# Block sums and the value products of batch 0 on the whole array, in a sparse-attention and expert-mixture kernel

## The chip, the cores and the metric

The kernel runs on one core of one Trainium2 chip. The metric is the device time of one execution in microseconds. Before the change it is 678.07 us, the median of three runs from 675.09 to 680.74 us. The profiled execution is one more execution, and its page gives its span, from the first to the last instruction: 673.4 us.

## The reference

Two things are computed one after the other. First comes attention for 4 batches of 8 heads with 768 positions of 64 numbers: every query sees its neighbours within 15 positions, and beside them 24 summaries, one for each block of 32 keys, whose value is the mean of the block's values.

```python
k_sum = k.reshape(B, H, nb, block, D).max(axis=3)      # block = 32, nb = 24
v_sum = v.reshape(B, H, nb, block, D).mean(axis=3)
scores_l = scale * np.matmul(q, k.transpose(0, 1, 3, 2))
mask_l = np.abs(pos[:, None] - pos[None, :]) < 16
scores_s = scale * np.einsum('bhsd,bhnd->bhsn', q, k_sum) + np.log(block)
a = softmax of [where(mask_l, scores_l, -1e9), scores_s]
out = a @ concatenate([v, v_sum])
```

Its output, 3072 rows of 512, goes through eight experts of 1024 hidden units. A gate of eight numbers a row is normalised eight times by rows and by columns and weighs the experts:

```python
P = np.exp(logits - logits.max())
for _ in range(8):
    P /= P.sum(1, keepdims=True); P /= P.sum(0, keepdims=True); P *= N / E
for e in range(8):
    out += P[:, e:e + 1] * (np.maximum(x @ w1[e], 0.0) @ w2[e])
```

## The kernel before, in words

**Stages.** The kernel has three stretches. The first does the attention together with expert 0 (`hidden0` and `project0`, lines L200 and L210), the second is a bridge with the normalisation of the gate (`sink`, L1117) and the first groups of expert 1, and the third goes through experts 1 to 7 in a loop written out by hand (L907 and L913). The change touches the first stretch alone, and by its planner also the bridge.

**Units.** Attention works on 16 pairs of heads, four for each batch, and 768 positions are six tiles of 128. Pairs 0 to 3 (batch 0, `PB` = 4) go in two halves of three tiles each (`pair_half`), all others as a whole (`pair_whole`). The steps of a pair are: keys and queries are transposed into `tkq` (L302 and L289 for batch 0, L305 later, and by DMA for the last pairs), copied out as `kT` and `qT` (L196); block maxima of the keys, `ksT` (L328); scores in `sg` (L334, in two PSUM banks of which there is one set), exponential on ScalarE (L458, L377), a band mask on VectorE (L463 and L468, later L383); scores of the summaries in `ss` (L420, L430) and their exponential (L441); block sums of the values in `vs` (L342), copied into `Vs` or `Ve` (L349); the value products in `av` (L479, later L406 and L412); normalisation (L509, L510); a transpose into `tx` (L517) and a copy into `xT` (L196), which is what expert 0 and the gate read.

**Shapes on TensorE.** Most products use 128 rows and 128 columns of the array. Some use a part: the scores have a contraction of 64, so that the two heads lie in two row halves (64x128); the transposes of batch 0 and `vs` put out 64 columns (128x64); `ss` is 64x32. The value products of one half pair in batch 0 (`values_h`) take three forms: six products of 128x128 for the tiles themselves, ten of 32x32 for the edges (the last or first 32 keys of a neighbouring tile against the first or last 32 queries), and three of 64x128 for the summaries. Each adds into the same bank `av`.

**Order.** A planner, class `Plan`, writes the instructions of all engines in the order of a list schedule: each unit has a cost on its engine, a list of units that it depends on, a priority and the PSUM buffers that it opens. Of the units that could start within 0.02 us of the earliest, the one with the lowest priority number goes first. Attention comes before expert 0, whose units fill what is left of TensorE; until the first unit of expert 0 is done, idle time of TensorE is filled with products of zeros (`keep_busy`, L555). Each engine then executes its own queue strictly in that order. The loads of q, k, v and weights all go out on GpSimd's queue, the transposes by DMA and the neighbour values (L362, L364) on SyncE's. `constants` is one unit on VectorE at the start; it is followed there by the identity and the band, of which GpSimd makes the rest (L572, L565, L567) between two loads.

Of the kernel before, what the change touches and what calls it, by code (L numbers as in the profile page):

```python
# [18 lines left out]
class Unit:  # L19
# [3 lines left out]
    def __init__(self, eng, cost, fn, deps, prio, opens, lag):  # L23
        self.eng = eng if isinstance(eng, dict) else {eng: cost}
        self.fn, self.deps, self.prio, self.opens, self.lag = fn, deps, prio, opens, lag
        self.start = self.end = self.on = None
# [7 lines left out]
class Plan:  # L34

    HOP = 0.15

    def __init__(self, slots, idle=None):
        self.slots, self.idle = {}, idle
        self.ring, self.turn, self.free, self.waiting = {}, {}, {}, []  # L40
        self.more(slots)
# [5 lines left out]
    def add(self, eng, cost, fn, deps=(), prio=0.0, opens=(), uses=(), lag=0.0):  # L47
        u = Unit(eng, cost, fn, [d for d in deps if d is not None], prio, list(opens), lag)
        for b in list(opens) + list(uses):
            b.users.append(u)  # L50
        if uses and eng != "PE":
            u.prio -= 100.0
        self.waiting.append(u)
        return u

    def order(self):
# [13 lines left out]
        while waiting or left:  # L70
# [4 lines left out]
            for u in left:  # L75
                t0 = ready(u)
                if t0 is None:
                    continue
                for e, cost in u.eng.items():
                    t = max([t0, free.get(e, 0.0)]  # L80
                            + [d.end + d.lag + (self.HOP if d.on != e else 0.0) for d in u.deps])
                    best.setdefault(e, []).append((t, u, cost))
            picks = []
            for e, c in best.items():
                t_min = min(t for t, _, _ in c)
                t, u, cost = min((x for x in c if x[0] <= t_min + 0.02), key=lambda x: x[1].prio)
                picks.append((t, t + cost, e, u, cost))
            t, end, e, u, cost = min(picks, key=lambda x: x[:2])
            if self.idle is not None:
# [3 lines left out]
                while self.idle is not None and t > free.get("PE", t) + us:  # L93
# [9 lines left out]
                    x.on = "PE"  # L103
# [4 lines left out]
            free[e] = end  # L108
            for b in u.opens:
                ring[b.tag][turn[b.tag] % self.slots[b.tag]] = b  # L110
                turn[b.tag] += 1
# [5 lines left out]
def kernel(  # L117
# [23 lines left out]
    W = 16  # L141
    LIVE = 128 + 2 * W
    PADL = LIVE + 2 * W
    HS = S // 2
    HG = G // 2
    VD = D + 1
    NEH = 3
# [78 lines left out]
    if True:  # L226
# [4 lines left out]
        m_blk = attn.tile([128, G, 64], BF16, name="m_blk")  # L231
# [4 lines left out]

        E_h = [attn.tile([128, 2, HG + 1, PADL], BF16, name=f"Eh{i}") for i in range(NEH)]
        V_s = [attn.tile([64, 2 * VD], BF16, name=f"Vs{i}") for i in range(PB)]
# [98 lines left out]

        def block_sums(i):
            sv = v_x[i % NQ]
            vs = at["vs", i] = bank("a", "vs")[0:64, 0:2 * D]  # L340
            for g in range(G):
                nc.tensor.matmul(vs.rearrange("p (j d) -> p j d", j=2), lhsT=m_blk[:, g, :],  # L342
                                 rhs=sv[:, :, g, 0:D], start=(g == 0), stop=(g == G - 1))
# [13 lines left out]
        def near_values(i):  # L357

            sv, ve = v_x[i % NQ], V_e[i % NE]
            for j in range(2):  # L360
                c0, q0 = VD * j, 64 + 32 * j
                nc.sync.dma_start(out=ve[q0 + W:q0 + 2 * W, 1:G, c0:c0 + VD],  # L362
                                  in_=sv[128 - W:128, j, 0:G - 1, :])
                nc.sync.dma_start(out=ve[q0:q0 + W, 0:G - 1, c0:c0 + VD],  # L364
                                  in_=sv[0:W, j, 1:G, :])
# [34 lines left out]
        def values(i, h):  # L400
            sv, ee, ve, em = v_x[i % NQ], E_e[i % NE], V_e[i % NE], at["em", i]
            av = at["av", i, h] = bank("a", "av")
            for cc in range(HG):
                c, o = HG * h + cc, cc * 2 * VD
                for j in range(2):
                    nc.tensor.matmul(av[:, o + j * VD:o + (j + 1) * VD],  # L406
                                     lhsT=em[:, j, c, :], rhs=sv[:, j, c, :],
# [26 lines left out]
        def summary_exp(i, h):  # L434
            o = 64 * h if i >= PB else 0
            if i < PB:
                es = at["es", i, h] = attn.tile([64, HG, 128], BF16, tag="es", name="es", bufs=2)
                dst = es[:]
# [21 lines left out]

        def masks_h(i, h):
            er, em = at.pop(("er", i, h)), E_h[(PB * h + i) % NEH]
            nc.vector.tensor_tensor(  # L463
                out=em[:, :, 0:HG, W:W + LIVE],
                in0=er[:, :, 0:HG * LIVE].rearrange("p j (g l) -> p j g l", l=LIVE),
                in1=band[:, None, None, :].to_broadcast([128, 2, HG, LIVE]), op=ALU.mult)
            p0, l0 = ((0, 0), (96, LIVE - W))[h]
            nc.vector.tensor_tensor(  # L468
                out=em[p0:p0 + 32, :, HG, W + l0:W + l0 + W],
                in0=er[p0:p0 + 32, :, HG * LIVE:HG * LIVE + W],  # L470
                in1=band[p0:p0 + 32, None, l0:l0 + W].to_broadcast([32, 2, W]), op=ALU.mult)

        def values_h(i, h):
            sv, em, es = v_x[i % NQ], E_h[(PB * h + i) % NEH], at.pop(("es", i, h))
            av = at["av", i, h] = bank("a", "av")

            def mm(p0, p1, cc, j, lhsT, rhs, n=VD, start=False, stop=False):
                o = cc * 2 * VD + j * VD
                nc.tensor.matmul(av[p0:p1, o:o + n], lhsT=lhsT, rhs=rhs, start=start, stop=stop,  # L479
                                 skip_group_check=True)  # L480

            for cc in range(HG):
                for j in range(2):
                    mm(0, 128, cc, j, em[:, j, cc, 2 * W:2 * W + 128], sv[:, j, HG * h + cc, :],
                       start=(cc == 0 and j == 0))
            for cc in range(HG):
                c = HG * h + cc
                for j in range(2):
                    if c + 1 < G:
                        mm(96, 128, cc, j, em[0:32, j, cc + 1, 0:32], sv[0:32, j, c + 1, :])  # L490
                    if c > 0:
                        mm(0, 32, cc, j, em[96:128, j, cc - 1 if cc else HG, LIVE:PADL],
                           sv[96:128, j, c - 1, :])
            for cc in range(HG):
                mm(0, 128, cc, 0, es[:, cc, :], V_s[i][:], n=2 * VD, stop=True)


        def normalize(i, h):
            av = at.pop(("av", i, h))[:, 0:HG * 2 * VD].rearrange("p (c x) -> p c x", x=VD)
# [6 lines left out]
            if i >= PB:  # L506
                t = t[:, HG * h:HG * (h + 1), :, :]
            rc = attn.tile([128, G, 1], FP32, tag="rc", name="rc", bufs=2)
            nc.vector.reciprocal(out=rc[:, :, 0], in_=av[:, :, D])  # L509
            nc.vector.tensor_tensor(out=t.rearrange("p g j d -> p (g j) d"), in0=av[:, :, 0:D],  # L510
                                    in1=rc[:].to_broadcast([128, G, D]), op=ALU.mult)
# [64 lines left out]

        def constants():
# [9 lines left out]
            for t in E_h:  # L587
                nc.vector.memset(t[:, :, :, 0:W], 0.0)
                nc.vector.memset(t[:, :, :, W + LIVE:], 0.0)
# [3 lines left out]
            for pq in range(4):  # L593
                for o in (pq, 32 + pq):
                    nc.vector.memset(flat[32 * pq:32 * pq + 32, o:o + 68 * (G - 1) + 1:68], 1.0)
# [41 lines left out]
        def pair_start(i, prio):  # L637
# [4 lines left out]
            for z in range(2 if i >= PB else 1):  # L642
                if i >= 12:
# [7 lines left out]
                                    prio, opens=[buf])  # L651
# [7 lines left out]
            U["vs", i] = add("PE", 0.4, lambda: block_sums(i),  # L659
# [4 lines left out]
        def query_half(i, h, prio):  # L664
# [3 lines left out]
                                opens=[buf])  # L668
# [4 lines left out]
        def pair_half(i, h, prio):  # L673
            if h:
                query_half(i, 1, prio)
            n = PB * h + i
            hold = U["A", PB - 1, 0] if h else None
            buf = Buffer("s")
            U["S", i, h] = add("PE", 0.36, lambda: scores_h(i, h),
                               [U["kT", i, 0], U["kT", i, 1], hist("mk", n - 3), hold], prio, opens=[buf])  # L680
            U["X", i, h] = add("ACT", 1.0, lambda: score_exp_h(i, h), [U["S", i, h]], prio, uses=[buf])
            U["mk", i, h] = add("DVE", 0.78, lambda: masks_h(i, h),
                                [U["X", i, h], U["band"], hist("A", n - NEH)], prio)
# [3 lines left out]
                                [U["km", i], U["kT", i, 1], hist("A", n - 2), hold], prio, opens=[buf])  # L687
            U["sx", i, h] = add("ACT", 0.46, lambda: summary_exp(i, h), [U["ss", i, h]], prio, uses=[buf])
            buf = Buffer("a")
            U["A", i, h] = add("PE", 0.65, lambda: values_h(i, h),  # L690
# [11 lines left out]
        def pair_whole(i, prio):  # L702
            U["near", i] = add("SP", 2.5, lambda: near_values(i), [U["v", i], U.get(("A", i - NE, 1))], prio,
                               lag=1.9)
            for h in range(2):
                buf = Buffer("s")
                U["S", i, h] = add("PE", 0.28, lambda h=h: scores(i, h),
                                   [U["kT", i, 0], U["kT", i, 1], U.get(("ed", i - 2))], prio, opens=[buf])
# [6 lines left out]
            U["ss", i, 0] = U["ss", i, 1] = add("PE", 0.22, lambda: summaries2(i),  # L715
                                                [U["km", i], U["kT", i, 1], U.get(("A", i - NE, 1))], prio,
                                                opens=bufs)
# [3 lines left out]
            for h in range(2):  # L721
                buf = Buffer("a")
                U["A", i, h] = add("PE", 0.4, lambda h=h: values(i, h),
# [570 lines left out]
```

## Time and profile before

| | |
|---|---|
| median of three runs | 678.07 us (675.09 to 680.74) |
| span of the profiled execution | 673.4 us |
| TensorE busy | 663.9 us, 99% of the span |
| VectorE busy | 580.2 us, 86% |
| ScalarE busy | 402.5 us, 60% |
| GpSimd busy | 131.5 us, 20% |
| granted TensorE clock | 0.999 over the span |
| first product of expert 0 (L200) starts at | 25.34 us |
| first product of L913 (end of the bridge) starts at | 168.68 us |

The span is 4.6 us under the median of the runs; the page does not give that execution's own device time, so a difference worked out in the span is carried over to the median as it stands. Matmuls are pipelined: a row's mean time is the time of one matmul from issue to end, several of them overlap, and the cost of a stream is read from the distance between the starts.

### The profile page before, as it was taken

The page shows a single profiled execution, that of the slowest core. Times are in us where ns is not written, and L with a number is a line of the kernel's source. Part 1 is how long each engine was busy: PE and PEld are TensorE (multiplying, and loading weights), DVE is VectorE, ACT ScalarE, POOL GpSimd, SP SyncE. Part 2 cuts the span into 40 slices and gives each one's busy share as a digit, 9 for nine tenths or more (in the row PEclk, how much of TensorE's full clock was granted, in tenths as well). Part 3 has the DMA queues.
Part 4 walks back from the last instruction along what each step waited for, and adds up shares of the span by engine and source line. Part 5 has one row for each costly group of instructions (what it writes and reads, how often), then busy time and mean ns, then how long its engine had stood idle before and what let it go on. Part 6 is the DMA issues. An engine that isn't in the chain of part 4 may idle for free.

```text
span 673.4 us, 13531 instructions
## 1 busy us (share of the span) xinstructions
PE 663.9 (99%) x5111; PEld 434.8 (65%) x5111; DVE 580.2 (86%) x1433; ACT 402.5 (60%) x783; POOL 131.5 (20%) x177
## 2 busy tenths in 40 slices
PE   8999999999999999999999999999999999999996
PEld 4666655555666666666666666666666666666665
DVE  6878889777799988998899988998899889998885
ACT  4777776565777765555655565555555555556552
POOL 8599622122101010201010010101020101100001
PEclk9999999999999999999999999999999999999999
DMA  9999959000513060311422050405031141201224
GB/s 115 190 147 145 151 85 172 2 1 1 79 11 37 1 79 1 36 14 21 59 22 28 1 78 9 40 1 79 1 33 17 20 60 20 30 0 48 82 91 158
DMA packets 124018, 36.46 MB, mean 54 GB/s; under 512 B 110384, under 2 KB 121136, under 8 KB 123952
## 3 DMA queue, kind: packets, MB, share of 16 engines
q0 software_dynamic: 104672, 26.22, 41.8%
q1 hardware_dynamic: 18464, 8.83, 5.6%
q8 instruction: 40, 0.66, 0.4%
q10 hardware_dynamic: 816, 0.54, 0.2%
q14 instruction: 26, 0.21, 0.1%
HBM read 52.45 MB, written 6.29 MB: 87 GB/s over the span
## 4 chain that ended last, share of the span: by engine, by line
PE 93%; DVE 4%; DMA 1%; POOL 1%; issue 1%; ACT 0%; DVEq 0%; ACTq 0%
PE xy L913 36%; PE pg L907 16%; PE pa L907 11%; PE pb L907 11%; PE hps L200 6%; PE yps L210 6%; PE sg L334 1%; DMA kst<-in_k_dram 1%; DVE hf L857 1%; PE tkq L305 1%; PE vs L342 1%; PE av L406 1%; PE av L412 1%; PE ss L430 1%; PE tx L517 0%
## 5 line engine op out<-in xcount | busy, mean ns | idle before, releaser
L913 PEld LDWEIGHTS <-hf 128*128 128x128 f16 x2352 | 230.1, 98 | 95.6 <-issue 0.5
L913 PE MATMUL xy<-w,hf 128*128 128x256 f16 x1312 | 183.4, 273 | 0.0
L913 PE MATMUL xy<-ws,hf 128*128 128x256 f16 x984 | 147.6, 273 | 0.1
L191 ACT ACTIVATE hf<-pg 128x512 f16<-128x512 f32 x84 | 50.2, 597 | 150.8 <-PE pg L907 150.8
L1049 DVE SCALAR_TENSOR_TENSOR out_acc<-xy,P_sb,out_acc 128x512 f32<-128x512 f32 x164 | 115.1, 744 | 2.1 <-PE xy L913 2.1
L854 DVE TENSOR_TENSOR hf<-hf 128x512 f16<-128x512 f16 x252 | 100.3, 424 | 8.8
L907 PE MATMUL pa<-xT,w 128*128 128x512 f16 x336 | 99.9, 379 | 0.0
L907 PEld LDWEIGHTS <-w 128*128 128x128 f16 x672 | 65.8, 98 | 44.4 <-issue 1.1
L857 DVE TENSOR_TENSOR hf<-pb,c 128x512 f16<-128x512 f32 x84 | 58.1, 692 | 38.5 <-PE pb L907 32.4
L176 POOL DMA_DIRECT2D w<-in_moe_w_dram x56 | 41.7, 754 | 220.6 <-PE pg L907 192.0
L907 PEld LDWEIGHTS <-ws 128*128 128x128 f16 x504 | 49.3, 98 | 25.3
L941 ACT COPY c<-pg 128x512 f32<-128x512 f32 x84 | 49.2, 586 | 22.4 <-PE pg L907 22.4
L857 DVE TENSOR_TENSOR hf<-pg,c 128x512 f16<-128x512 f32 x84 | 57.2, 681 | 0.8 <-PE pg L907 0.8
L926 ACT COPY pg<-pa 128x512 f32<-128x512 f32 x84 | 47.9, 570 | 4.8
L191 ACT ACTIVATE hf<-pa 128x512 f16<-128x512 f32 x84 | 50.6, 602 | 0.0
L907 PE MATMUL pg<-xTs,w 128*128 128x512 f16 x168 | 50.0, 379 | 0.2
L907 PE MATMUL pg<-xT,w 128*128 128x512 f16 x168 | 50.0, 379 | 0.1
L907 PE MATMUL pb<-xT,ws 128*128 128x512 f16 x168 | 50.0, 379 | 0.0
L907 PE MATMUL pb<-xTs,ws 128*128 128x512 f16 x168 | 50.0, 379 | 0.0
L907 PE MATMUL pg<-xTs,ws 128*128 128x512 f16 x168 | 50.0, 379 | 0.0
L934 ACT COPY c<-pb 128x512 f32<-128x512 f32 x84 | 49.8, 592 | 0.0
L200 PE MATMUL hps<-xT,w 128*128 128x384 f16 x256 | 48.6, 326 | 0.0
(141 smaller groups left out, 820.1 us busy)
## 6 DMA issues: line engine op xcount, KB each, us to landing
w<-in_moe_w_dram POOLq DMA_DIRECT2D x8, 1024.0 KB, 8.9
w<-in_moe_w_dram POOLq DMA_DIRECT2D x56, 128.0 KB, 3.5
out_dram<-out_acc SPq DMA_DIRECT2D x20, 256.0 KB, 2.0
qst<-in_q_dram POOLq DMA_DIRECT2D x32, 96.0 KB, 5.7
vx<-in_v_dram POOLq DMA_DIRECT2D x16, 192.0 KB, 6.5
kst<-in_k_dram POOLq DMA_DIRECT2D x24, 96.0 KB, 5.9
w<-in_moe_w_dram POOLq DMA_DIRECT2D x2, 512.0 KB, 8.6
kst<-in_k_dram POOLq DMA_DIRECT2D x4, 192.0 KB, 5.1
```

The lines of the kernel that those rows point to most:

```text
L176: nc.gpsimd.dma_start(out=t[:, :, h, :], in_=moe_w1[e].rearrange("(dk p) f -> p dk f", p=128)[:, :, f:f + 128])
L191: nc.scalar.activation(out=out, in_=in_, func=AF.Relu, bias=0.0, scale=1.0)
L200: nc.tensor.matmul(hp[:, 0:n], lhsT=w1s[e][:, dk, 128 * f:128 * (f + 1)], rhs=xT[:, dk, t0:t0 + n], start=(dk == 0), stop=(dk == KD - 1))
L210: nc.tensor.matmul(yp[:], lhsT=h[:, f, c * 128:(c + 1) * 128], rhs=w2s[e][:, f, :], start=(f == 0), stop=(f == KF - 1))
L854: nc.vector.tensor_tensor(out=out, in0=in0, in1=in1, op=ALU.subtract)
L857: nc.vector.tensor_tensor(out=out, in0=in0, in1=in1, op=ALU.add)
L907: nc.tensor.matmul(bank[:], lhsT=w[:, dk, :], rhs=x[:, dk, :], start=start and dk == 0, stop=dk == KH - 1, skip_group_check=True)
L913: nc.tensor.matmul(bank, lhsT=a(f)[:, 128 * c:128 * (c + 1)], rhs=w[:, f, :], start=start and f == 0, stop=f == FH - 1, skip_group_check=True)
L926: nc.scalar.copy(out=B["g"][:], in_=B["a"][:])
L934: nc.scalar.copy(out=B["c5"][:], in_=B["b"][:])
L941: nc.scalar.copy(out=B["c2"][:], in_=B["g"][:])
L1049: nc.vector.scalar_tensor_tensor(out=acc, in0=src, scalar=P_sb[:, t, e:e + 1], in1=acc, op0=ALU.mult, op1=ALU.add)
```

## The change

Three parts. First, the block sums (`block_sums`) get a 0/1 matrix `m_blk` of 128 columns instead of 64, so that their product is 128x128; rows 64 to 127 of the result are not read. Second, `values_h` computes everything with 128x128 products: the masked scores `E_h` get 112 zero columns around each stretch of 160 live ones, and an edge product takes a window of 128 columns in which only the live end is not zero, over all 128 keys of the neighbouring tile; the exponentials of the summaries go into two lasting tiles `E_s` whose lower half is zero, and `V_s` gets 128 rows. The zeros are written once, by `pads`: for the first of the three `E_h` tiles within `constants`, for the two others as units of their own on VectorE. The edge mask covers 128 partitions instead of 32. Third, units on TensorE carry a shape, the planner adds `RESHAPE` = 0.1 us to a unit whose shape differs from that of the last one, and of units that are ready together it takes one with a shape after another one with a shape; some costs are set anew. `normalize` is written with other views of the same data.

```diff
+    RESHAPE = 0.1
...
                 for e, cost in u.eng.items():
+                    if e == "PE" and u.shape != self.shape:
+                        cost += self.RESHAPE
...
-                t, u, cost = min((x for x in c if x[0] <= t_min + 0.02), key=lambda x: x[1].prio)
+                t, u, cost = min((x for x in c if x[0] <= t_min + 0.02), key=lambda x: (
+                    not (e == "PE" and self.shape and x[1].shape), x[1].prio))
...
-    PADL = LIVE + 2 * W
+    PAD = 128 - W
+    ROW = PAD + HG * (LIVE + PAD) + W + PAD
...
-        m_blk = attn.tile([128, G, 64], BF16, name="m_blk")
+        m_blk = attn.tile([128, G, 128], BF16, name="m_blk")
...
-        E_h = [attn.tile([128, 2, HG + 1, PADL], BF16, name=f"Eh{i}") for i in range(NEH)]
-        V_s = [attn.tile([64, 2 * VD], BF16, name=f"Vs{i}") for i in range(PB)]
+        E_h = [attn.tile([128, 2, ROW], BF16, name=f"Eh{i}") for i in range(NEH)]
+        E_s = [attn.tile([128, HG, 128], BF16, name=f"Es{i}") for i in range(2)]
+        V_s = [attn.tile([128, 2 * VD], BF16, name=f"Vs{i}") for i in range(PB)]
...
-            vs = at["vs", i] = bank("a", "vs")[0:64, 0:2 * D]
+            vs = at["vs", i] = bank("a", "vs")[:, 0:2 * D]
...
+        def live(c):
+            return PAD + c * (LIVE + PAD)
+
...
             for cc in range(HG):
                 for j in range(2):
-                    mm(0, 128, cc, j, em[:, j, cc, 2 * W:2 * W + 128], sv[:, j, HG * h + cc, :],
-                       start=(cc == 0 and j == 0))
+                    mm(cc, j, live(cc) + W, HG * h + cc, start=(cc == 0 and j == 0))
...
                     if c + 1 < G:
-                        mm(96, 128, cc, j, em[0:32, j, cc + 1, 0:32], sv[0:32, j, c + 1, :])
+                        mm(cc, j, live(cc + 1) + W - 128, c + 1)
                     if c > 0:
-                        mm(0, 32, cc, j, em[96:128, j, cc - 1 if cc else HG, LIVE:PADL],
-                           sv[96:128, j, c - 1, :])
+                        mm(cc, j, live(cc - 1) + W + 128 if cc else live(HG), c - 1)
             for cc in range(HG):
-                mm(0, 128, cc, 0, es[:, cc, :], V_s[i][:], n=2 * VD, stop=True)
+                o = 2 * cc * VD
+                nc.tensor.matmul(av[:, o:o + 2 * VD], lhsT=E_s[(PB * h + i) % 2][:, cc, :], rhs=V_s[i][:],
+                                 start=False, stop=True, skip_group_check=True)
...
+        def pads(n):
+            t = E_h[n]
+            nc.vector.memset(t[:, :, 0:PAD], 0.0)
+            nc.vector.memset(t[:, :, live(0):live(HG)].rearrange("p j (g l) -> p j g l", l=LIVE + PAD)[:, :, :, LIVE:],
+                             0.0)
+            nc.vector.memset(t[:, :, live(HG) + W:], 0.0)
...
-            for t in E_h:
-                nc.vector.memset(t[:, :, :, 0:W], 0.0)
-                nc.vector.memset(t[:, :, :, W + LIVE:], 0.0)
+            pads(0)
+            for t in E_s:
+                nc.vector.memset(t[64:128, :, :], 0.0)
...
+            clear = add("DVE", 0.65, lambda: pads(n), [c0], prio - 0.5) if 0 < n < NEH else None
...
-                               [U["kT", i, 0], U["kT", i, 1], hist("mk", n - 3), hold], prio, opens=[buf])
+                               [U["kT", i, 0], U["kT", i, 1], hist("mk", n - 3), hold], prio, opens=[buf], shape="row")
...
-            U["A", i, h] = add("PE", 0.65, lambda: values_h(i, h),
+            U["A", i, h] = add("PE", 0.67, lambda: values_h(i, h),
```

## The prediction

> **What bounds the kernel.** I read the page's busy times and its chain first. TensorE is busy 99% of the span and makes up 93% of the chain that ended last.
>
> ```profile
> PE 663.9 (99%) x5111; PEld 434.8 (65%) x5111; DVE 580.2 (86%) x1433; ACT 402.5 (60%) x783; POOL 131.5 (20%) x177
> ...
> PE 93%; DVE 4%; DMA 1%; POOL 1%; issue 1%; ACT 0%; DVEq 0%; ACTq 0%
> ```
>
> Busy time alone can hide gaps, since a matmul's end is modelled, so I asked next what TensorE waited for from the first product of expert 0 (25.34 us) to the end of the bridge (168.68 us):
>
> ```profile
> PE sink L1117 <- DVE csum_sb L1112: 0.8, 1, 0.8
> PE ss L430 <- DVE xT L196: 0.5, 1, 0.5
> ```
>
> The columns are total, times and longest. Two waits, 1.3 us of 143. There TensorE's queue is the bound: every nanosecond of TensorE work removed comes off the end, and everything that follows (pure matmul work as well) moves up. Before 25.34 us it is different: TensorE waits for loads and for other engines, and fills with zero products, so work removed there is worth nothing.
>
> Third, the timeline of TensorE in a piece of the middle stretch (start, busy, line, operation, count; a stream's cost is the distance to the next start):
>
> ```profile
> 41.56 1.89 PE L210 MATMUL yps<-w,h 128*128 128x512 f16 x8
> 43.39 0.38 PE L334 MATMUL sg<-qT,kT 64*128 64x160 bf16 x6
> 43.70 0.53 PE L342 MATMUL vs<-vx,m_blk 128*64 128x128 bf16 x6
> 44.16 1.04 PE L210 MATMUL yps<-w,h 128*128 128x512 f16 x4
> 45.03 0.35 PE L406 MATMUL av<-vx,em 128*128 128x65 bf16 x6
> 45.22 0.34 PE L412 MATMUL av<-Ve,Ee 128*128 128x130 bf16 x3
> ```
>
> Four `yps` products before `av`, same shape, take 45.03 - 44.16 = 0.87 us, 0.217 each; eight before `sg`, which has another shape, take 1.83, that is 0.09 more than 8 x 0.217. The single starts of the trace say it more sharply: `hps` to `hps` 162 ns, `hps` to `sg` 258; `yps` to `yps` 216, to `ss` 309; `vs` to `yps` 151, where two products of 128 elements stand 56 apart. **A change of shape costs 0.095 us**, whichever the two shapes are.
>
> **The changed work on TensorE.** I counted changes of shape in the order of instructions of both programs up to the end of the bridge: 141 before, 105 after. From the first product of expert 0 on, where they count, there are 100 and 72. So 28 x 0.095 = -2.66 us. One half pair of batch 0 shows where the fewer come from:
>
> ```profile
> 31.68 0.65 PE L479 MATMUL av<-vx,Eh 128*128 128x65 bf16 x16
> 32.26 0.34 PE L479 MATMUL av<-Vs,es 64*128 64x130 bf16 x3
> 32.53 1.47 PE L200 MATMUL hps<-xT,w 128*128 128x384 f16 x8
> ```
>
> From 31.68 to 32.53 three shapes follow each other, with a change before the ten edges, after them, and before `hps`.
>
> The edges get dearer. Nine distances between the ten 32x32 products make 172 ns, 19 each. The padded ones are 128x128 with 65 columns out, each with weights of its own, which is L406's form: 29 to 30 ns apart over 120 neighbours. Four of eight half pairs lie behind 25.34 us: 40 x 10.5 ns = +0.42 us. The three summary products stay at some 59 ns.
>
> The block sums: 72 products lie behind 25.34 us. Starts within `vs` are 62 ns apart on the mean, while `tx` with 128x128 and 128 elements shows 56. So 0 to -0.4 us; I take -0.2, the middle. The weight load of `vs` (64 columns) lasts 108 ns in the trace, that of 128 columns 98. The Trainium skill's page "TensorEngine Tiling (Array Packing)", under Restrictions, says that column tiling switches the fast weight load off, which would explain that odd order. By that rule the whole -0.4 would come, and the sum would be 0.2 us lower.
>
> One score unit now stands ahead of the first product of expert 0 instead of behind it: -0.30 us (a half pair's scores, 31.09 to 31.41 in the timeline).
>
> TensorE work behind the first product of expert 0: -2.66 + 0.42 - 0.2 - 0.30 = **-2.74 us**.
>
> **Waits there.** The first `sink` waits 0.8 us because only four expert products (0.65 us) stand between the start of the bridge and it. In the new order it is four and twelve more (0.65 + 2.59 us), so I take -0.8. The 0.5 us at `ss` may go or come back elsewhere: bounds 0 and -1.3 together. New waits are a rival below.
>
> **The start.** Here the change adds. GpSimd's second load stands in its queue behind the making of the identity, which waits for VectorE:
>
> ```profile
> 4.71 0.29 POOL L572 TENSOR_SCALAR_AFFINE_SELECT ident<-ident 128x128 bf16<-128x128 bf16 x1 [0.70 <-DVE ident L571]
> 4.95 0.72 POOL L262 DMA_DIRECT2D kst<-in_k_dram  x1
> ```
>
> VectorE clears the identity at 4.52 us, directly after `constants`. That unit gets longer. The rows: a memset of 384 words (L604) lasts 378 ns, one of 192 (L591) 218, so 0.83 ns a word and about 22 ns more from start to start; the six old ones of `E_h` stand 75 ns apart, 0.45 us together. Added are 560 words in three (0.53 us), two of 192 for `E_s` (0.36) and 192 more for `m_blk` (0.16): 1.05 - 0.45 = +0.60 us. All of GpSimd's later loads are issued 0.60 us later. How much of that reaches the keys of pair 3, the last of batch 0, is not in the trace: their arrival releases TensorE at 17.70 us,
>
> ```profile
> 17.70 0.53 PE L302 MATMUL tkq<-ident,kst 128*64 128x128 bf16 x12 [0.45 <-DMA kst<-in_k_dram]
> ```
>
> and the load was issued at 10.49, so for 7 us the DMA engines and not the issue were behind. Bounds 0 and 0.6; I take 0.4, as the first loads have been done by the time the second one's packets start. The other two `pads` (1.06 us) stand on VectorE where it idles from 5.23 to 6.64, and hold up the first query copy by some 0.4 us; the next keys are awaited anyway, so 0.
>
> From those keys to the first product of expert 0 there is a chain: transpose, copy, scores, exponential, mask, values, normalisation, transpose, copy. Before it takes 25.34 - 17.70 = 7.64 us. The new order puts three things into it: pair 3's queries are copied on ScalarE behind the key copy (0.80) instead of beside it on VectorE: 0.5 us; a copy into `xT` (0.3 to 0.36) stands ahead of the mask, partly in a wait; and the last copy into `xT`, here ahead of two query copies (the two lines of VectorE)
>
> ```profile
> 25.19 0.29 DVE L196 COPY xT<-tx 128x384 f16<-128x384 f16 x1
> 25.40 1.00 DVE L196 COPY qT<-tkq 128x384 bf16<-128x384 bf16 x2
> ```
>
> comes behind both, +1.1 us, of which TensorE has less to wait because that copy is read only by the fourth product. I take +1.2 us for the chain; bounds 0.3 (only the score unit that now runs in it) and 1.9 (all three in full). The start costs 0.4 + 1.2 = **+1.6 us**, between 0.3 and 2.5.
>
> **Edits at nothing.** The edge mask over 128 partitions: its time goes by elements per partition, which stay 32 (154 to 172 ns). `normalize`: same elements out of PSUM (557 ns). SyncE: one key transpose (1.21 us) now goes ahead of four neighbour loads (0.59 each) whose reader is far behind, two other moves are among transposes; TensorE's waits name no such DMA, and without that cover it would be 1.2 us. GpSimd's queue keeps its order.
>
> **The sum.** -2.74 - 0.8 + 1.6 = -1.94 us on the profiled span of 673.4, and so on the median of 678.07: **676.1 us**. With all terms at one end: -2.66 + 0.42 - 0.30 - 0.4 - 1.3 + 0.3 = -3.9 (674.1), and -2.54 + 2.5 = 0 (678.0). The runs of before scatter by -3.0 and +2.7 us around their median, so 1% (6.8 us) is about what a measurement tells from no change.
>
> **Rivals.**
>
> A. The start costs nothing beyond the 0.3 us and both waits go: -2.74 - 1.3 + 0.3 = -3.7, **674.3 us**. For it: VectorE idles in the chain for DMA. Against: the copy order, which is fixed in the queue. 13%.
>
> B. Slower: scores wait. There is one set of score banks (`NS` = 1), so a score unit needs the exponential of the last one finished (0.31 + 0.97 us and the two hand-overs, about 1.6). With the instruction order and the distances above, successive score units stand 1.7 us apart or more before; after, the closest late in attention are 1.59, 1.64, 1.69 and 1.69, and nine in all under 2.1. TensorE's queue is strict, so an instruction of ScalarE in between (a copy of `out_acc`, 0.58 us) stops it and all of expert 0 behind it. Nine times 0.6 is 5.4 us: -1.94 + 5.4 = +3.5, **681.6 us**. It decides from 1.94 us of such waits, 0.22 each. For it: the nearer distances. Against: no score unit waited at 1.7. 15%.
>
> C. The change doesn't do what it says, because the stretch isn't bound by TensorE but by the chain through VectorE (84 to 96% busy between 50 and 110 us), and shape changes only fill gaps. Then what VectorE gets is paid, 0.6 + 1.06 us of memsets less what lies in its idle time: about +0.6, **678.7 us**. Against: the two waits in 143 us. 8%.
>
> D. Weight loads pace the padded edges. A 128-column load lasts 98 ns; if they did not overlap, 40 x (98 - 29.5) ns = +2.7 us, **678.8 us**. Against it are 120 neighbours of L406 at 29 to 30 ns with new weights each. 4%. The Trainium skill's page "TensorE: Matmul & The Clock Gate", under Back-to-back issue gap, has this rule: in a stream of load and matmul pairs both set the pace, some 81 ns a product at 128 columns. By it alone the 40 would cost about 2.1 us more than I count; the trace disagrees, with 56 ns for that size (`tx`).
>
> **Range and chances.** The forecast has 60%. Its terms reach from 674.1 to 678.0, A lies inside, C and D just above; the scatter of the runs, with three to a median, widens that to about 672.2 and 680.2, which leaves most of B out. Faster by over 1% (under 671.3) needs more than every term at its end: 3%. Slower by over 1% (over 684.8) needs B at double its price: 4%. Within 1%: 93%.
>
> **What would show it.** In the profile after: `av` of L491 as one run of sixteen 128x128 products 29 to 30 ns apart and no 32x32 form; `vs` 128x128, 56 ns apart, and no 0.095 us between it and `yps`; the first product of expert 0 near 26.9 us; the first of L913's (now L931) near 166.7; no wait at the first `sink`. I am wrong if score units show waits of over 0.2 us each, if the first product of expert 0 comes after 28 us, or if the edges stand further apart than 30 ns.

## The result, and the profile after

The changed kernel takes 679.19 us (median of 20 runs, 676.67 to 682.18), the kernel before 676.08 us (20 runs, 674.20 to 680.74). The ratio is **1.0041, with a 95% interval from 1.0027 to 1.0055**: slower by 0.4%, where 0.3% faster was forecast. The profiled execution agrees: its span goes from 673.4 to 676.2 us.

The page of the kernel after, busy times and the chain that ended last:

```profile
PE 662.3 (98%) x5108; PEld 435.5 (64%) x5108; DVE 580.7 (86%) x1438; ACT 401.6 (59%) x783; POOL 131.4 (19%) x177
...
PE 89%; DMA 4%; DVE 4%; POOL 1%; issue 1%; ACT 0%; SPq 0%; DVEq 0%; ACTq 0%
```

TensorE has less to do (662.3 us against 663.9) and the kernel takes longer. The chain says where to look: TensorE's share falls from 93% to 89%, and DMA's rises from 1% to 4%.

The products themselves came out as drawn up. A half pair in the timeline of TensorE after (start, busy, line, operation, count):

```profile
29.11 0.66 PE L491 MATMUL av<-vx,Eh 128*128 128x65 bf16 x16
29.61 0.33 PE L506 MATMUL av<-Vs,Es 128*128 128x130 bf16 x3
29.78 0.33 PE L527 MATMUL tx<-ident,xs 128*128 128x128 f16 x3
```

Sixteen products take 29.61 - 29.11 = 0.50 us, and no change of shape lies in or behind them. Over 120 neighbours the distance in L491 is 29 ns at the median (30.9 on the mean); in `vs` (L353) it is 57 ns at the median; `vs` to `yps` or `hps` is 56 to 57 ns, without the 0.095 us.

A sum over both traces places the loss. Each product from the first of expert 0 (`hps`) to the first of the third stretch (`xy`, L931) is given the undisturbed distance of its kind of neighbours; what the stretch takes beyond that sum is waiting, time at half the clock, and what the method can't place (before, 2.50 us stand against 1.3 us of listed waits). The sums are estimates, since they depend on how the neighbours are grouped.

| us | before | after | difference | forecast |
|---|---|---|---|---|
| start to TensorE's first product on the keys of pair 3 | 17.70 | 18.05 | +0.35 | +0.4 |
| from there to the first `hps` | 7.64 | 8.31 | +0.67 | +1.2 |
| `hps` to `xy`: TensorE's work | 140.85 | 138.40 | -2.45 | -2.74 |
| `hps` to `xy`: beyond the work | 2.50 | 7.18 | **+4.68** | **-0.8** |
| `xy` to the last product | 499.56 | 499.14 | -0.42 | 0 |

The start up to pair 3's keys and TensorE's work were near the forecast, the chain behind the keys grew by about half of its forecast, and the waits have the wrong sign. What TensorE waited for between 26.3 and 172 us after (total, times, longest):

```profile
PE tx L527 <- DVE xs L520: 2.7, 2, 2.5
PE lp L541 <- DVE xs L520: 0.9, 1, 0.9
PE av L423 <- DVE Ve L364: 0.2, 1, 0.2
PE av L423 <- DMA Ve<-vx: 0.2, 1, 0.2
```

The two waits of before are gone, the one at the first `sink` as forecast, and others have come. They lie in the tail of attention. The timeline of TensorE there:

```profile
102.54 0.76 PE L541 MATMUL lp<-wg_bf,xT 128*128 128x8 f16 x24 [0.95 <-DVE xs L520]
...
111.98 2.11 PE L208 MATMUL hps<-xT,w 128*128 128x384 f16 x12
...
116.58 0.50 PE L527 MATMUL tx<-ident,xs 128*128 128x128 f16 x3 [2.49 <-DVE xs L520]
...
117.28 0.50 PE L527 MATMUL tx<-ident,xs 128*128 128x128 f16 x3 [0.19 <-DVE xs L520]
117.57 2.46 PE L208 MATMUL hps<-xT,w 128*128 128x384 f16 x8
```

Twelve `hps` take 2.11 us, but eight of them 5 us later take 2.46. The stretches of this trace show why (window: length, TensorE busy and count, granted clock, DMA share, GB/s):

```profile
110.00:112.00 2.00, 2.00 (x27) 1.00 1.23 192
113.50:117.00 3.50, 1.01 (x7) 0.88 0.83 63
117.00:119.60 2.60, 2.41 (x11) 0.50 0.02 6
120.00:122.00 2.00, 2.00 (x34) 1.00 0.00 0
```

After the wait the granted clock is 0.50; `hps` stand 320 ns apart instead of 162. So the wait of 2.5 us is paid with about another 1.3 us behind it (eight `hps`, 0.16 us each).

VectorE's normalisation (`xs`, L520), which these transposes (`tx`) need, is itself waiting. VectorE's waits from 85 to 125 us after, of which before has none of this kind:

```profile
DVE xs L520 <- DMA xT<-xs: 4.8, 3, 3.0
```

And the chain of that piece after (start, length, what):

```profile
104.51 0.84 DVE em L394 x2
105.35 10.17 DMA xT<-xs
115.52 0.03 issue
115.55 0.02 DVEq L520
115.57 0.40 issue
115.97 0.56 DVE xs L520
116.53 0.11 DVE rc L519
116.64 0.02 issue
116.66 0.57 DVE xs L520
117.23 0.05 issue
117.28 0.50 PE tx L527 x3
117.78 2.26 PE hps L208 x8
```

There are two `xs` tiles for the late pairs. Pair 15's normalisation needs the one that pair 13's transpose by DMA is still reading. That transpose is issued at 105.35 us and lands 10.17 us later, and everything below it in the chain follows from that. In the same piece before, the chain is TensorE alone, and pair 15's normalisation starts without a wait. The row before and the row after:

```profile
118.94 0.56 DVE L510 TENSOR_TENSOR xs<-av,rc 128x384 f16<-128x384 f32 x1
```

```profile
115.97 0.56 DVE L520 TENSOR_TENSOR xs<-av,rc 128x384 f16<-128x384 f32 x1 [2.96 <-DMA xT<-xs]
```

The reason is not that transposes were fast before. The transposes and weights in the DMA views of 85 to 125 us, first before, then after, and the weight loads on GpSimd in the same order:

```profile
DMA to landing us min/median/max: 2.8/4.9/8.4
```

```profile
DMA to landing us min/median/max: 4.4/6.0/10.2
```

```profile
98.46 5.95 POOL L176 DMA_DIRECT2D w<-in_moe_w_dram  x8 [0.28 <-issue]
```

```profile
96.20 5.94 POOL L184 DMA_DIRECT2D w<-in_moe_w_dram  x8 [0.28 <-issue]
```

Slow they were before too, up to 8.4 us, beside the loads of expert 1's weights; but the old order leaves room. Before, pair 13's transpose is issued at 108.70 us and pair 15's normalisation starts at 118.94, 10.2 us later, directly behind its value products (118.15). After, the transpose is issued at 105.35, 3.4 us earlier, but the value products of pair 15 start at 111.26, 6.9 us earlier; VectorE is ready for the normalisation at 113.01, 7.7 us behind the issue, and then waits 2.96 us.

The landing moved less than the issue. In the traces this transpose lands just behind the last of expert 1's first weight loads: before, the weights are in at 116.59 us and the transpose at 117.14; after, at 115.32 and 115.52. So the landing came 1.6 us forward and its reader 5.9, and the difference of 4.3 us is more than the 1.8 us that were left between the landing and the reader before. The new order has used up a reserve that no list of waits before names, since nothing waited there.

At the start, VectorE clears the identity 1.00 us later (5.52 against 4.52), and GpSimd's second load leaves 1.00 us later (5.95 against 4.95). TensorE starts on pair 3's keys 0.35 us later. But the trace has these keys landed at 17.46 us after, against 17.66 before, although their load was issued 0.99 us later: no part of the later issue shows in their landing. What TensorE waits for ahead of them is a load of values (0.74 us, until 17.03). Timelines of GpSimd and TensorE after:

```profile
5.71 0.29 POOL L582 TENSOR_SCALAR_AFFINE_SELECT ident<-ident 128x128 bf16<-128x128 bf16 x1 [1.68 <-DVE ident L581]
5.95 0.72 POOL L271 DMA_DIRECT2D kst<-in_k_dram  x1
```

```profile
18.05 0.53 PE L311 MATMUL tkq<-ident,kst 128*64 128x128 bf16 x12
```

### The profile page after: what moved, and what is told of

Read it like the earlier page. It is cut to its first block, busy times and chain, and to the rows that moved or that the text cites. A ratio compares the mean times of both kernels' runs of the same rounds, so it can differ in the third digit from the quotient of the medians.

```text
span 676.2 us, 13534 instructions
## 1 busy us (share of the span) xinstructions
PE 662.3 (98%) x5108; PEld 435.5 (64%) x5108; DVE 580.7 (86%) x1438; ACT 401.6 (59%) x783; POOL 131.4 (19%) x177
## 4 chain that ended last, share of the span: by engine, by line
PE 89%; DMA 4%; DVE 4%; POOL 1%; issue 1%; ACT 0%; SPq 0%; DVEq 0%; ACTq 0%
PE xy L931 36%; PE pg L925 16%; PE pa L925 11%; PE pb L925 11%; PE hps L208 5%; PE yps L218 5%; DMA xT<-xs 2%; DMA Ve<-vx 1%; DMA vx<-in_v_dram 1%; PE tkq L314 1%; PE sg L343 1%; DVE xs L520 1%; PE tx L527 1%; PE vs L353 0%; PE av L423 0%
## 5 line engine op out<-in xcount | busy, mean ns | idle before, releaser
L931 PEld LDWEIGHTS <-hf 128*128 128x128 f16 x2352 | 230.1, 98 | 95.9 <-issue 0.8
L931 PE MATMUL xy<-w,hf 128*128 128x256 f16 x1312 | 183.4, 273 | 0.0
L931 PE MATMUL xy<-ws,hf 128*128 128x256 f16 x984 | 147.6, 273 | 0.1
```

What stands on the lines that cost most here:

```text
L931: nc.tensor.matmul(bank, lhsT=a(f)[:, 128 * c:128 * (c + 1)], rhs=w[:, f, :], start=start and f == 0, stop=f == FH - 1, skip_group_check=True)
```

## The experiments

**The theory** after that comparison: the tail of attention asks for results of DMAs earlier than they come while expert 1's weights are being loaded. **Its rivals**: the two `xs` tiles alone are the limit; the planner's assumed time for a transpose is; late weights are a gain of their own, whatever the order; one part of the change, the products or the planner, is the dear one. The start is tested apart. All ratios are against the kernel before, which was measured again beside each group of kernels; the kernel after was not, so comparisons with it go through the kernel before.

### Room in one place: a third tile, and a longer assumed transpose

A third `xs` tile for the late pairs (paid for with one buffer of `erh`), same order on TensorE:

```diff
-  ... tag="erh", name="erh", bufs=3)
+  ... tag="erh", name="erh", bufs=2)
-  tag=f"xs{i < PB}", name="xs", bufs=2)
+  tag=f"xs{i < PB}", name="xs", bufs=2 if i < PB else 3)
```

> The changed kernel with three xs tiles for the later batches instead of two (room made by two instead of three tiles for the exponentials of batch 0); the order of every TensorE instruction is unchanged. T1: the normalisations of pairs 14 and 15 no longer wait for DMA (0.9 and 3.0 us on VectorE go), the transposes of pair 15 are ready at about 114 us; what is late next is the landing of the last DMA transpose, which the last logits need at about 115 to 117 us. So 2 to 5 us less than the changed kernel: 674 to 677 us, ratio 0.997 to 1.001. T2 and T3: ratio 1.004.

Measured: 675.87 us, ratio 0.9995 (0.9978 to 1.0013). What TensorE waits for from 26.3 to 172 us in this kernel:

```profile
PE av L423 <- DMA Ve<-vx: 2.5, 1, 2.5
PE tkq L314 <- DMA kst<-in_k_dram: 0.5, 1, 0.5
PE lp L541 <- DMA xT<-xs: 0.5, 1, 0.5
```

The waits for `xs` are gone, and the next DMA in line is late: the neighbour values of the last pairs, which take up to 8.5 us beside the weights. Here the clock stayed at 1.00 behind the wait. So the tiles are the first limit, not the only one.

The second kernel leaves everything but tells the planner that a transpose by DMA takes 9.5 us:

```diff
-                                             lag=4.5)
+                                             lag=9.5)
```

> The changed kernel with one number altered: the planner takes 9.5 us instead of 4.5 us for the landing of a transpose of x by DMA. Same products, same 105 changes of shape, the same TensorE work from the first product of expert 0 on (138.4 us by the distances of the starts); only the order of the tail differs: the last logits come 9 us of TensorE work later (114.3 instead of 105.2). Theory T1 (the loss is waits in the tail of attention, where the normalisation waits for a DMA transpose to free one of two xs tiles, and TensorE's strict queue behind it): the 5.7 us of waits between 101 and 120 us go nearly all, time 679.2 - 5 = 674 us, ratio to before 0.996 to 0.998. Theory T2 (the padded products and what VectorE gets cost more than counted, in any order): as the changed kernel, ratio 1.004. Theory T3 (the start alone): ratio 1.003 to 1.004 too.

Measured: 677.57 us, ratio 1.0000 (0.9980 to 1.0021), where 0.996 to 0.998 was expected. Its waits in the same window:

```profile
PE av L423 <- DMA Ve<-vx: 2.8, 3, 1.1
PE sink L1135 <- DVE csum_sb L1130: 1.9, 2, 1.4
PE pg L925 <- DVE xT L872: 0.8, 1, 0.8
```

The planner now puts attention's last steps later (the bridge starts at 127.06 us instead of 121.12), so that less of expert 0 is left to fill the chain of `sink`. The wait has changed its place and its name. The profiled execution is this kernel's slowest run (679.19 us), so its waits may be larger than those of the median run.

### Taking the crowding away

Expert 1's weight loads wait until pair 14's transpose has landed; GpSimd's copy of one element is the wait:

```diff
         def hold():
             ...
+            nc.gpsimd.tensor_copy(out=held[0:1, 0:1], in_=xT[0:1, 14 % PB, 3 * S:3 * S + 1])
-        last[0] = add("POOL", 0.3, hold, [last[0]] + [U["kT", i, 1] for i in range(12, NP)])
+        last[0] = add("POOL", 0.3, hold, [last[0]] + [U["kT", i, 1] for i in range(12, NP)] + [U["x", 14]])
```

> The changed kernel with the loads of expert 1's weights held back until the last DMA transpose of x has landed; TensorE's order is the same but for the first zero products of the bridge. It asks why a transpose took 10.2 us in the tail where an earlier one took 5.1. T1 with crowding (the weights' packets are in the way): transposes of pairs 12 to 14 land in 5 to 6 us, VectorE's wait of 3.0 us goes, 3 to 5 us less than the changed kernel (674 to 676 us), if the weights then come in time for the bridge. T1 without crowding (the neighbour loads ahead of it on SyncE's queue set the time): the transposes still take 8 to 10 us and the time stays at 679, or more if the weights come late.

Measured: 673.20 us, ratio 0.9943 (0.9922 to 0.9964), faster than the 674 to 676 us expected. The transposes from 85 to 125 us and TensorE's waits from 26.3 to 172:

```profile
DMA to landing us min/median/max: 2.7/2.9/4.7
```

```profile
PE av L423 <- DMA Ve<-vx: 2.0, 2, 1.5
```

The same five transposes land in 2.9 us at the median instead of 6.0. Every wait for `xs` is gone, and the 2.0 us that are left end at 43.4 and 91.7 us, ahead of the tail. By the two ratios, 0.98% has come back against the kernel after, by one wait on GpSimd, whose next work is those loads.

Is that a gain of late weights as such? The same edit on the kernel before:

> The kernel before, with the loads of expert 1's weights held back until the last DMA transpose of x has landed, as in late_w. Theory T1 (the change saves TensorE work and loses it again because its order asks for the tail's DMA results earlier than crowded queues deliver them): the order of before covers those landings, so holding back the weights gains next to nothing here: ratio 0.998 to 1.003 (676 to 679 us), the last if the weights then come late for the bridge. Rival T4 (weights that come later are a gain in themselves, and late_w says nothing of the change): ratio 0.994, as late_w.

Measured: 676.05 us, ratio 0.9995 (0.9976 to 1.0015), with these waits:

```profile
PE ss L430 <- DVE xT L196: 0.5, 1, 0.5
PE xy L914 <- DVE crec_sb L1121: 0.3, 1, 0.3
```

No gain, although the five transposes now land after 2.9 us at most: nothing had waited for them. That rival falls: here late weights are worth something only to an order that asks early.

### The parts of the change

The whole-array products alone: no charge for a change of shape, the old rule of choice and the old costs.

```diff
-    RESHAPE = 0.1
+    RESHAPE = 0.0
-  ... key=lambda x: (not (e == "PE" and self.shape and x[1].shape), x[1].prio))
+  ... key=lambda x: x[1].prio)
```

> The whole-array products alone: the planner's charge, its rule of choice and its new costs are taken back. 107 changes of shape instead of 141, 75 instead of 100 from the first product of expert 0; TensorE work there 138.9 us against 140.9 before. The last logits stand at 113.2 us of TensorE work, near the 115.6 of before. T1: the start costs 1 us, the work saves 2.0, tail waits 0 to 2: ratio 0.9985 to 1.002. T2: ratio 1.004, as the changed kernel.

Measured: 676.17 us, ratio 0.9994 (0.9974 to 1.0014). The changes of shape up to the end of the bridge are 107 (75 behind the first `hps`), against 105 (72) with the new planner: the products remove nearly all of them by themselves. But this kernel waits in the tail too, longest for the transpose that the gate's logits read:

```profile
PE lp L540 <- DMA xT<-xs: 2.1, 1, 2.1
PE sink L1134 <- DVE csum_sb L1129: 0.8, 1, 0.8
PE ss L440 <- DVE xT L203: 0.7, 1, 0.7
```

The planner's part alone, on the products of before, with the new costs (a half pair's value products at 0.84 us, for the changes of shape inside them):

> The kernel before with the planner's part alone (charge of 0.1 us for a change of shape, the rule of choice, the new costs; block sums count as 128x64 and a half pair's values as ending at 64x128). 133 changes of shape instead of 141, 95 instead of 100 from the first product of expert 0; TensorE work there 140.4 against 140.9 us. The last logits stand 2.7 us of TensorE work earlier. T1: half a us saved, 0 to 3 us of waits for DMA in the tail: ratio 0.999 to 1.004. If the charge by itself were the loss: 1.004 or more.

Measured: 676.32 us, ratio 0.9991 (0.9975 to 1.0007). Its profiled execution can't be set against the others piece by piece, since its start ran at a low clock (columns as above):

```profile
15.00:20.00 5.00, 5.00 (x68) 0.50 1.59 186
20.00:25.00 5.00, 5.00 (x52) 0.50 1.37 200
```

Its tail can be read. TensorE's waits from 29.5 to 173 us:

```profile
PE tx L524 <- DVE xs L517: 1.3, 3, 0.7
```

In this trace too VectorE's normalisation of pair 15 waits 2.0 us for pair 13's transpose, which takes 10.6 us. Each part alone measures as no change, and both together as +0.41%. The parts do not add up. That both draw on the same reserve in the tail fits the two traces; it is not shown by a run.

The products alone with late weights, the counterpart of the kernel with both parts and late weights:

> The whole-array products without the planner's part, with the weights held back. T1: the one wait of 2.1 us for a DMA transpose (at the third batch's or last logits) goes, and the 2.0 us of saved work shows: 673.5 to 675 us, ratio 0.995 to 0.998. T4: ratio 0.993 to 0.994, about as late_w. If the planner's part is worth nothing, it ties with late_w.

Measured: 673.08 us, ratio 0.9948 (0.9930 to 0.9966), beside 0.9943 with the planner's part: a tie. Against the kernel before with late weights it is 0.47% faster, some 3 us, where the products by themselves save 2.0 us of TensorE's work. Part of the 3 us is the clock: three of the twelve runs of the kernel before with late weights have a mean granted clock of 0.990 to 0.993, none of the six here is under 0.997. Among runs at 0.998 and more the means are 674.7 (five) and 673.0 us (four), 1.6 us apart. So the saving is there, in about its size, and the crowded tail swallowed it.

### The start

The identity and the band are written first among VectorE's constants, on the kernel after:

```diff
+        nc.vector.memset(ident, 0.0)
+        nc.vector.memset(band, 1.0)
         ... (the other constants)
-            nc.vector.memset(ident, 0.0)
-            nc.vector.memset(band, 1.0)
```

> The kernel after the change, in which VectorE clears the identity and sets the band ahead of the other constants; nothing else. Late weights and this edit together took 1.74 us more off than late weights alone (673.20 to 671.46 us), and the first product of expert 0 came 2.1 us earlier. Theory 1: the start is a cost of its own and all behind the first product of expert 0 is bound by TensorE's queue except the tail, whose waits are set by transposes and weight loads. The weight loads of expert 1 start when pair 14's queries have been read on TensorE, so they move up with everything else, and the waits in the tail stay: about -1.7 us against the kernel after the change, some 677.5 us beside 679.2, and a ratio of about 1.0015 against the kernel before. Rival: the waits in the tail are set by something that does not move with the start, and eat what the start gains: about 679 us, ratio 1.004.

Measured: 676.89 us, ratio 0.9995 (0.9975 to 1.0015). The first `hps` starts at 24.19 us instead of 26.36, but the first `xy` only at 170.82 instead of 171.94: in the trace the stretch up to there takes back 1.1 of 2.2 us. The median stands 2.3 us under that of the kernel after, more than the 1.7 us expected. With late weights as well:

> late_w, and the clearing of identity and band moved ahead of constants on VectorE, so that GpSimd's second load no longer waits for the longer constants. The start theory: identity ready near 2 us instead of 5.7, the second load issued at 4.0 instead of 5.95 us, the keys of pair 3 at 17.0 to 17.7 instead of 18.05 to 18.4, the first product of expert 0 at 25.7 to 26.2 instead of 26.7: 0.4 to 1.0 us less than late_w, 672.2 to 672.8 us, ratio 0.992 to 0.994. If DMA engines and not the issue set the arrival, nothing: 673.2.

Measured: 671.46 us (671.04 to 672.22), ratio **0.9926 (0.9907 to 0.9945)**, the fastest kernel of this study, 0.74% under the kernel before, and faster than the 672.2 to 672.8 us expected. GpSimd's timeline at its start:

```profile
4.09 0.32 POOL L583 TENSOR_SCALAR_AFFINE_SELECT ident<-ident 128x128 bf16<-128x128 bf16 x1
4.34 0.74 POOL L271 DMA_DIRECT2D kst<-in_k_dram  x1
```

The second load leaves 1.61 us earlier than after, and with it all loads behind it. The second load itself lands no earlier (9.66 us against 9.22), but the keys of pair 3 land at 15.87 against 17.46, TensorE starts on them at 16.13 against 18.05, and the first `hps` starts at 24.55 against 26.36. So the issue of the loads behind the identity does reach the end of the start. The last of the series puts both edits on the products alone:

> The whole-array products with the old planner, the weight loads of expert 1 held back until the transpose by DMA of pair 14 has landed, and the identity and the band ahead of the other constants. The first two gave 673.08 us together. If the start is a cost of its own, as with the changed planner, 1.0 to 1.7 us less: 671.4 to 672.1 us, which ties with the same edits on the changed planner (671.46). If the gain at the start belongs to the changed planner's order alone, 673 us.

Measured: 672.27 us, ratio 0.9939 (0.9917 to 0.9962). That lies between the two expectations. The interval overlaps that of the kernel with the planner's part, so that part is again worth nothing that shows. Its first `hps` comes 1.36 us earlier than with late weights alone, but the first `xy` at 166.18 instead of 166.11: of the gain at the start nothing is left in this trace, with 0.6 us of it at `sink`, where no wait was.

## Why the prediction was wrong, point by point

**The changed work on TensorE: right.** 28 changes of shape fewer were counted, as in the trace after, and at 0.095 us each they make up most of the fall; the work fell by 2.45 us instead of 2.74. The 0.29 us between are not placed: the edges at 30.9 ns on the mean instead of 29.5 account for some 0.06. With 128 columns the weight load of `vs` lasts 96 ns instead of 108. That agrees with the rule of the Trainium skill's page "TensorEngine Tiling (Array Packing)", under Restrictions, that column tiling switches the fast weight load off. The products of `vs` stand 58 ns apart on the mean instead of 62, while the medians hardly differ (57 and 57.5), since a few distances of 82 ns went; over 72 products that is 0.3 us beside the 0.2 taken. Rival D did not hold: the products stand 57 ns apart at 128 columns and 29 at 65, with new weights each. The 81 ns at 128 columns of the Trainium skill's page "TensorE: Matmul & The Clock Gate", under Back-to-back issue gap, does not agree with these 57 ns; the prediction had put it on the edges too, which stream only 65.

**The start: right in kind.** +1.02 us instead of +1.6. Two terms of it were mis-sized. `constants` grew by 1.00 us and not 0.60, because its instructions stand further apart than the rows made them: the three of `E_h` take 0.71 us up to the next one instead of 0.53, the two of `E_s` 0.55 instead of 0.36; the chain behind the keys grew by 0.67 and not 1.2. The +0.35 beside the forecast of +0.4 is luck: the keys themselves landed 0.2 us earlier than before, and other loads held TensorE up. The step "for 7 us the DMA engines and not the issue were behind" holds for that 1.00 us, and not in general: with the identity first and nothing else, pair 3's keys landed at 15.17 us instead of 17.46, and TensorE started on them at 15.82 instead of 18.05. Nor is +1.02 us a sharp number: the kernel before and the kernel before with late weights have the same start, and their first `hps` stand at 25.34 and 26.12 us, the second with a stretch at half the clock in its start.

**Waits there: this step failed.** "I take -0.8", with bounds of 0 and -1.3, and "New waits are a rival below". Both old waits went, as said. In their place came 4.0 us of listed waits, nearly all for results that a DMA held up, and about 1.3 us behind the longest with TensorE at half its clock. Put in the forecast's own sum, -2.45 + 4.68 + 1.02 - 0.42 = +2.83, which is the span's +2.8. The step had looked at the waits of before and asked which of them would go; it put new waits for DMA at nothing, and did not ask how much time each DMA of the tail had left before its reader came. Rows of before would have told that: pair 13's transpose took 8.4 us to land, its tile was needed 10.2 us behind the issue, so 1.8 us were left, and the new plan moves the reader 5.9 us forward (its value products 6.9) and the issue only 3.4. Under **Edits at nothing** stands the sentence that carried this: "TensorE's waits name no such DMA". It is true, and it says only that the reserve was not yet used up.

**The rivals.** B, slower by waits, had the right sign and the wrong resource: no score unit waited, though their distances shrank as worked out. C did not hold either, as the kernel with late weights shows; TensorE's queue is the bound again once the tail's DMAs come in time. C's 678.7 us and D's 678.8 stand nearest to the measured 679.19, but by luck. The mechanism that decided was not among the four, and none of the three signs of being wrong that the prediction named asks for it.

**The sum and the base.** The forecast was carried to a median of three runs, 678.07; 20 runs give 676.08. A forecast of -1.94 on that base is 674.1. So the predicted 676.1 stands further from the truth than the 3.1 us that it seems to miss: the error of the difference is some 4.8 us in the spans (+2.8 instead of -1.94). The base could have been seen: in all eleven kernels where both are known, the device time of the profiled execution is 1.7 to 1.9 us above its span, so the 673.4 us of before stand for about 675.1 us, an estimate, and not for the median.

**What stays open.** Why the products alone, with 2.1 us for the transpose and a slow clock behind it, measure 0.47% under both parts together, where the two traces differ by 1.0 us only. The profiled executions explain part of it: 677.95 us is below the median of the one kernel (679.19), 676.97 above that of the other (676.17). The clock does not: the mean granted clock over the runs is 0.9965 and 0.9962. For the kernel before the clock does go with the time: of its 76 runs beside the experiments, those under 676 us have 0.998 to 1.000, those over 678 us 0.990 to 0.997; where its clock falls in these is not known. How much of the +0.41% belongs to the occasion is open too, since the kernel after was not run again: all eight kernels made from it by a further edit, even the one told 9.5 us, came out at 1.0000 or below. Whether the gain in the sum comes without the holding of the weights, by another order of the neighbour loads, wasn't tried.

## What to carry to other kernels

Where a change makes the bounding engine's work shorter, or lets a planner move its steps, list for every DMA that it waits on when the transfer landed in this place, beside which other loads, and how long after that its reader came; a reader that moves up by more than that, against the landing, turns the saving into a wait, and no list of waits shows that in advance. Such a wait is not cured where it appears: a third tile or another assumed time moved it to the next transfer, while taking the weight loads out of the way removed it. And when two parts of a change measure as nothing each and as a loss together, look for a reserve that both may draw on.

## What the runs showed of the hardware

**Transposes by DMA beside loads.** The same transpose lands after 2.9 us at the median with expert 1's weights held back (4.7 at most), and after 6.0 (10.2 at most) beside them; neighbour loads go from 2.1 to 4.5 us. In the seven kernels that load the weights beside it, pair 13's transpose was issued between 105.1 and 112.8 us and landed 0.2 to 0.6 us behind the last of these weight loads each time. Which of the two holds up the other the traces don't tell; with the weights held back it lands after 2.8 us.

**The clock falls after short waits, for a fixed time.** In the traces, up to the last product, the granted clock falls to 0.50 for 3.41 us or a whole number of such steps: behind a wait in the kernel after (from 116.18 us), in the products alone (from 106.01) and in the kernel with the identity first (from 103.14), and for four steps, 13.65 us, at the start of the planner's part alone. The stretches at full clock ahead of the first three are whole numbers of these steps too (32, 29 and 29), as if the clock were set on a fixed grid. In the step just before the fall TensorE was busy for 1.32, 1.28 and 1.99 us of 3.41. Stretches of the kernel with the identity first, around its fall:

```profile
100.00:102.60 2.60, 1.19 (x26) 1.00 1.62 153
102.80:106.60 3.80, 3.80 (x19) 0.55 2.46 174
```

With three tiles 2.5 us of waiting left the clock at 1.00; there the wait lies across two steps, with 2.08 and 2.28 us of busy time. Busy time alone does not decide it: with the identity first, a step with 1.65 us (from 113.38) was followed by no fall. The Trainium skill's page "TensorE: Matmul & The Clock Gate", in Part 1 on the clock gate, gives an idle window of about 3.4 us as what takes the clock to half. The half rate agrees with the 320 ns here; a wait of that length was not needed in these runs, where TensorE idled for 2.1, 2.1 and 1.4 us of the step.
